# A fused transformer block on one core: second token blocks four pieces later, first halves' tiles ahead, and engines that may hold longer for urgent work

## The chip, the core and the metric

One core of a Trainium2 chip. The metric is the device time of one execution in microseconds (us), as the median of several. Six things work side by side on the core: TensorE (PE, with its weight loads as PEld), VectorE (DVE), ScalarE (ACT), GpSimd (POOL), SyncE (SP) and the DMA queues.

## The reference, cut to what matters

```python
x = A_x                                             # [1, 2048, 1024] bf16
h = x + linear_attention(layernorm(x), A_wqkv, A_wo)   # 32 heads, phi(t) = (t > 0 ? t + 1 : exp(t)) + 1e-6
g, u = layernorm(h) @ W_gate, layernorm(h) @ W_up      # F = 3584
h2 = h + (g * (g > 0) * u) @ W_down
```

## The kernel before

The big products are done in quads: seven products of half-size blocks in place of eight, from sums of blocks (the "left sums" of activations, sums of weights, sums of results). TensorE has 4163 matmuls; DVE and ACT move results out of PSUM, the memory that TensorE writes ("evict" them), make the sums and the norms; POOL scales and shifts normalised tiles; the SP queue transposes them by DMA. Tokens come in tiles of 128. `s` is the block of tokens, `i` the half, `tt` the tile in it. Tiles T0 to T7 belong to the first blocks, T8 to T15 to the second.

The program first records every instruction as a node, then a list scheduler lays them out ahead of time with estimated durations (`hold`), and they are issued in that order. Each engine then runs its own list strictly in order. `late` is the latest start that does no harm.

```python
# Plan.schedule(): the next engine to be free, and its most urgent ready instruction i
now = [i for i in a if nodes[i].ready <= s]
i = min(now, key=lambda i: (nodes[i].nom if e == "tensor" else nodes[i].late, i))
v = nodes[i]
if e != "tensor":
    soon = [j for j in a if s < nodes[j].ready < s + 0.5 * v.hold and nodes[j].late < v.late - 1500.0]
    if soon:                       # hold the engine for something more urgent
        i = min(soon, key=lambda j: (nodes[j].late, j))
        v = nodes[i]
        s = v.ready
v.start = s
clock[e] = s + v.hold
# ... (ends, DMA and successors: cut)

tiles = [Tile_(s, i, tt) for s in range(NS) for tt in range(SW // P) for i in range(2)]
# ... (steps() and the first blocks: cut)
t8, t9 = tiles[NTS:NTS + 2]
tick.units.extend([t8.nd01, None, t9.nd01, None, t8.nd2, t9.nd2] + steps(NTS, 2 * NTS, 2, 0, False)[4:])

def finish(self, on_dve=False):    # of a tile of the first norm
    self.rstd_()
    (nc.vector if on_dve else nc.gpsimd).tensor_scalar(out=xn, in0=self.x, scalar1=self.negm[:], scalar2=self.rstd[:],
                            op0=ALU.add, op1=ALU.mult)
    nc.sync.dma_start_transpose(out=XI[self.i][:, :, self.r:self.r + P], in_=xn)
```

`tick.units` is the list of pieces of attention work (`nd01`, `nd2`, `wo`) that are woven between the matmuls of the quads; a `None` is an empty turn.

## Time and profile before

| | before |
|---|---|
| median of 3 runs | 727.81 us (727.63 to 728.01) |
| the execution that was profiled | 726.09 us, span 724.3 us |
| PE busy | 714.4 us, 99% of the span |
| PE idle in its main group | 6.5 us |
| DVE, ACT, POOL busy | 563.9, 277.3, 77.8 us |

PE is nearly always busy, so the whole question is the handful of places where it isn't. The prediction below shows those lines; in a line of PE's timeline, the number in the brackets is how long PE stood idle before the stretch and the name after the arrow is what released it. The execution that was profiled took 1.7 us less than the median.

### The profile page before, as it was taken

The page shows a single profiled execution, that of the slowest core. Times are in us where ns is not written, and L with a number is a line of the kernel's source. Part 1 is how long each engine was busy: PE and PEld are TensorE (multiplying, and loading weights), DVE is VectorE, ACT ScalarE, POOL GpSimd, SP SyncE. Part 2 cuts the span into 40 slices and gives each one's busy share as a digit, 9 for nine tenths or more (in the row PEclk, how much of TensorE's full clock was granted, in tenths as well). Part 3 has the DMA queues.
Part 4 walks back from the last instruction along what each step waited for, and adds up shares of the span by engine and source line. Part 5 has one row for each costly group of instructions (what it writes and reads, how often), then busy time and mean ns, then how long its engine had stood idle before and what let it go on. Part 6 is the DMA issues. An engine that isn't in the chain of part 4 may idle for free.

```text
span 724.3 us, 11221 instructions
## 1 busy us (share of the span) xinstructions
PE 714.4 (99%) x4163; PEld 396.7 (55%) x4163; DVE 563.9 (78%) x954; ACT 277.3 (38%) x540; POOL 77.8 (11%) x88
## 2 busy tenths in 40 slices
PE   8999999999999999999999999999999999999998
PEld 4444545444444444444444444444444688888887
DVE  7897745887796885666767968769758879899996
ACT  5877555666554443333333333333333220001100
POOL 1342000002202110000000000000000004001452
PEclk9999999999999999999999999999999999999999
DMA  9556406069766630446145575685681878777974
GB/s 300 165 117 110 138 0 212 23 109 216 160 156 151 140 73 6 129 136 186 60 139 188 165 244 157 202 253 186 198 262 51 276 265 209 216 265 238 242 80 60
DMA packets 156503, 117.40 MB, mean 162 GB/s; under 512 B 54944, under 2 KB 140192, under 8 KB 156320
## 3 DMA queue, kind: packets, MB, share of 16 engines
q1 hardware_dynamic: 148832, 113.01, 53.9%
q0 software_dynamic: 7616, 3.67, 4.8%
q8 instruction: 32, 0.52, 0.3%
q14 instruction: 23, 0.19, 0.1%
HBM read 70.52 MB, written 34.08 MB: 144 GB/s over the span
## 4 chain that ended last, share of the span: by engine, by line
PE 85%; DVE 2%; DMA 2%; ACT 1%; issue 0%; POOL 0%; ACTq 0%
PE psum L122 85%; DVE mem L122 2%; DMA mem<-mem 2%; ACT mem L122 1%; POOL mem L122 0%; ACT tiny L122 0%; DVE tiny L122 0%; ACTq L122 0%
## 5 line engine op out<-in xcount | busy, mean ns | idle before, releaser
L122 PE MATMUL psum<-mem 128*128 128x512 f16 (+4 forms) x4147 | 713.3, 334 | 6.5 <-ACT mem L122 2.7
L122 PEld LDWEIGHTS <-mem 128*128 128x128 f16 (+1 forms) x4163 | 396.7, 98 | 323.8 <-issue 8.0
L122 DVE TENSOR_TENSOR mem<-psum,mem 128x512 f32<-128x512 f32 (+2 forms) x240 | 187.4, 794 | 99.3 <-ACT mem L122 65.1
L122 DVE TENSOR_TENSOR mem<-mem 128x512 f16<-128x512 bf16 (+8 forms) x400 | 241.6, 643 | 14.9 <-DMA mem<-mem 9.6
L122 ACT COPY mem<-psum 128x512 f32<-128x512 f32 (+2 forms) x124 | 92.7, 749 | 209.4 <-PE psum L122 197.9
L122 ACT COPY psum<-psum 128x512 f32<-128x512 f32 (+1 forms) x68 | 49.1, 722 | 160.3 <-PE psum L122 147.6
L122 POOL DMA_DIRECT2D out_dram<-mem x28 | 34.1, 1299 | 413.8 <-DVE mem L122 413.7
L122 ACT ACTIVATE mem<-psum 128x512 bf16<-128x512 f32 x90 | 53.6, 598 | 18.5 <-PE psum L122 18.0
L122 DVE SCALAR_TENSOR_TENSOR mem<-mem 128x512 bf16<-128x512 bf16 (+1 forms) x71 | 57.7, 813 | 1.3
L122 POOL TENSOR_SCALAR mem<-mem,tiny 128x1024 bf16<-128x1024 bf16 x28 | 37.5, 1338 | 196.9 <-ACT tiny L122 176.8
L122 DVE SCALAR_TENSOR_TENSOR mem<-psum,mem 128x512 bf16<-128x512 f32 x66 | 45.4, 688 | 11.9 <-PE psum L122 7.9
L122 ACT ACTIVATE mem<-mem,tiny 128x1024 bf16<-128x1024 bf16 x24 | 27.4, 1143 | 11.0 <-DVE tiny L122 5.8
L122 DVE TENSOR_SCALAR mem<-mem 128x512 bf16<-128x512 bf16 (+1 forms) x49 | 16.3, 332 | 17.6 <-ACT mem L122 17.4
L122 DVE TENSOR_TENSOR mem<-psum,tiny 128x384 bf16<-128x384 f32 (+1 forms) x48 | 22.9, 508 | 5.3 <-ACT tiny L122 3.9
L122 ACT ACTIVATE mem<-mem 128x1024 bf16<-128x1024 f32 (+1 forms) x23 | 24.3, 1056 | 6.5 <-DVE mem L122 6.4
L122 ACT ACTIVATE tiny<-tiny 128x1 f32<-128x1 f32 (+2 forms) x112 | 22.8, 206 | 7.5 <-DVE tiny L122 4.7
L122 ACT ACTIVATE tiny<-psum 128x12 f32<-128x12 f32 (+1 forms) x48 | 8.1, 169 | 13.9 <-PE psum L122 13.4
L122 DVE BATCH_NORM_STATS2 tiny<-mem 128x6 f32<-128x512 bf16 x16 | 10.2, 682 | 2.5 <-DMA mem<-in_A_x_dram 2.5
L122 ACT CAST mem<-psum 128x512 bf16<-128x512 f32 x18 | 10.4, 582 | 4.2 <-PE psum L122 3.7
L122 POOL TENSOR_SCALAR tiny<-tiny 128x1 f32<-128x1 f32 x14 | 4.7, 337 | 25.2 <-ACT mem L122 13.3
L122 ACT ACTIVATION_READ_ACCUMULATOR mem<-mem,tiny 128x1 f32 x24 | 4.5, 188 | 0.0
L122 DVE TENSOR_SCALAR tiny<-tiny 128x1 f32<-128x1 f32 x16 | 3.4, 210 | 0.3
(18 smaller groups left out, 14.4 us busy)
## 6 DMA issues: line engine op xcount, KB each, us to landing
l_dram<-mem SPq DMA_DIRECT2D x98, 128.0 KB, 2.2
mem<-l_dram SPq DMA_DIRECT2D x12, 896.0 KB, 6.4
mem<-in_A_x_dram SPq DMA_DIRECT2D x32, 256.0 KB, 3.0
mem<-in_B_W_up_dram SPq DMA_DIRECT2D x14, 512.0 KB, 5.3
mem<-in_B_W_gate_dram SPq DMA_DIRECT2D x14, 512.0 KB, 4.3
mem<-in_B_W_down_dram SPq DMA_DIRECT2D x28, 256.0 KB, 3.4
r_dram<-mem SPq DMA_DIRECT2D x56, 128.0 KB, 1.8
mem<-r_dram SPq DMA_DIRECT2D x8, 896.0 KB, 5.0
```

What stands on the lines that cost most here:

```text
L122: call = lambda: getattr(getattr(self.nc, eng), op)(*args, **k)
```

## The change

The intent: PE's waits are to go. Three edits, all to the order of work and none to the work. (1) Before 215 us of planned time an engine other than TensorE may be held, that is kept idle, for up to 1.2 times the length of the instruction it would start, not 0.5, where something more urgent is nearly ready. (2) The tiles of the first blocks go half by half. (3) The attention pieces of the second blocks start four turns later.

```diff
+    SHORT = 215000.0
...
-                soon = [j for j in a if s < nodes[j].ready < s + 0.5 * v.hold and nodes[j].late < v.late - 1500.0]
+                wait = (1.2 if s < self.SHORT else 0.5) * v.hold
+                soon = [j for j in a if s < nodes[j].ready < s + wait and nodes[j].late < v.late - 1500.0]
...
-    tiles = [Tile_(s, i, tt) for s in range(NS) for tt in range(SW // P) for i in range(2)]
+    tiles = [Tile_(0, i, tt) for i in range(2) for tt in range(SW // P)]
+    tiles += [Tile_(1, i, tt) for tt in range(SW // P) for i in range(2)]
...
-    tick.units.extend([t8.nd01, None, t9.nd01, None, t8.nd2, t9.nd2] + steps(NTS, 2 * NTS, 2, 0, False)[4:])
+    tick.units.extend([None] * 4 + [t8.nd01, None, t9.nd01, None, t8.nd2, t9.nd2] + steps(NTS, 2 * NTS, 2, 0, False)[4:])
```

## The prediction

> **What bounds the kernel now.** I read the page first, then the timeline of PE, then the busy time by stretch, then the short timelines of ACT and DVE around each gap of PE. The page:
>
> ```profile
> PE 714.4 (99%) x4163; PEld 396.7 (55%) x4163; DVE 563.9 (78%) x954; ACT 277.3 (38%) x540; POOL 77.8 (11%) x88
> ...
> L122 PE MATMUL psum<-mem 128*128 128x512 f16 (+4 forms) x4147 | 713.3, 334 | 6.5 <-ACT mem L122 2.7
> ```
>
> PE is busy 99% of a span of 724.3 us, and the chain that ended last is 85% PE. But "busy" with modelled ends may hide slack, so I check the pace: from 285 to 570 us the stretch view counts 1322 matmuls of 512 columns in 285.0 us, 215.6 ns each. Start to start, the trace has 215 or 216 ns for 512 columns, 109 for 256, 57 to 62 for 132. Taking each form's median as its pace, the 4163 matmuls need 709.9 us; first to last start they took 719.4. So only some 9.6 us of PE time are lost at all, 2.9 of them in the first 10 us. The timeline of PE (start, length, and in brackets idle before and its releaser) shows where:
>
> ```profile
> 28.76 25.68 PE L122 MATMUL psum<-mem 128*128 128x512 bf16 x140 [0.54 <-DVE mem L122]
> 55.01 94.85 PE L122 MATMUL psum<-mem 128*128 128x512 f16 x518 [0.57 <-ACT mem L122]
> 150.64 40.70 PE L122 MATMUL psum<-mem 128*128 128x512 bf16 x219 [0.78 <-DMA mem<-mem]
> 192.79 9.26 PE L122 MATMUL psum<-mem 128*128 128x512 bf16 x48 [1.46 <-ACT mem L122]
> 202.61 97.68 PE L122 MATMUL psum<-mem 128*128 128x132 bf16 x489 [0.56 <-DVE mem L122]
> ```
>
> Start to start the same five cost 0.70, 0.73, 0.94, 1.62 and 0.72 us (a matmul's modelled tail covers some 0.16 of each). Smaller hitches add 0.9 between 40 and 77 us, 0.3 at 127, 0.4 at 146 and 0.6 between 205 and 208. After 208.5 us PE runs at its pace to the end: nothing later can be gained, only lost. The stretches say what is full beside PE:
>
> ```profile
> 140.00:152.00 12.00, 11.16 (x67) 5.53 (x66) 11.76 (x24) 7.56 (x25) 0.00 (x0) 1.00 0.24 45
> 152.00:188.00 36.00, 36.00 (x199) 17.67 (x198) 26.23 (x67) 20.55 (x67) 8.87 (x7) 1.00 0.89 185
> 188.00:210.00 22.00, 19.82 (x108) 9.34 (x106) 20.55 (x41) 16.08 (x41) 1.19 (x1) 1.00 0.67 167
> 210.00:285.00 75.00, 75.00 (x378) 35.24 (x377) 58.03 (x117) 31.48 (x89) 9.81 (x8) 1.00 0.45 98
> ```
>
> The columns after the length are PE, PEld, DVE, ACT, POOL. Where PE loses time DVE is at 98% and 93%; between them it has 27% to spare. The short timelines tell the worst gap:
>
> ```profile
> 187.93 0.42 DVE L122 TENSOR_TENSOR mem<-mem 128x512 f16<-128x512 bf16 x1 [2.76 <-DMA mem<-mem]
> ...
> 189.60 1.06 ACT L122 ACTIVATE mem<-mem 128x1024 bf16<-128x1024 f32 x1 [1.15 <-DVE mem L122]
> 190.56 1.14 ACT L122 ACTIVATE mem<-mem,tiny 128x1024 bf16<-128x1024 bf16 x1
> ...
> 192.17 0.57 ACT L122 COPY mem<-psum 128x512 f32<-128x512 f32 x1
> ```
>
> DVE stood 2.76 us before a left-sum instruction whose transpose had not landed, with a PSUM eviction ready behind it; then ACT did a 1.06 us exponential and a 1.14 us square while the copy PE wanted (its products were done at 190.4) waited until 192.17.
>
> **What the Trainium skill says.** "TensorE: Matmul & The Clock Gate", section "Wait — 56ns, not 53.3ns?": N/2.4 GHz plus about 2.5 ns start to start when warm, 215.7 ns at 512 columns, 426.7 when cold. The trace agrees: 215 to 216, and about 427 for the first eight, so PE's pace can't be improved by this change. "Perfetto Trace Analysis", section "Identifying the Most-Contended Engine": PE busy time is a poor measure of how near PE is to its limit; hence the count by pace. Same page, section "Sequencer Loop": an instruction waits for its semaphores before it executes; the trace shows the consequence in the 2.76 us above, an engine waiting for one instruction with ready work behind it. "DMA: Bandwidth & Descriptors", section "Latency and other measured facts", gives about 2 us as the fixed cost of a DMA, growing with load; here transposes took 3.1 us (the one PE waits for at 150.64) and 5.0 us (182.95 to 187.9, with the DMA busy).
>
> **The change, part by part.** No matmul, eviction or transfer is added: the built programs have the same 4163 matmuls and 663 DVE rows in other orders. It all happens in the scheduler that orders instructions ahead of time. I compared the built orders and set the order of before against the trace by counting.
>
> (1) Before the scheduler's own 215 us, a non-PE engine may now hold up to 1.2 times an instruction's length, not 0.5, when something more urgent is about to be ready. At 28.76 PE waits for an add from PSUM (0.69 us at 28.02) behind two statistics instructions (1.28 us) that nobody needs soon; the new order has the add first. Gain: the whole 0.70. At 55.01 PE waits for an ACT copy (54.39) behind two tiny instructions which waited for DVE; the new order has the copy ahead of them. Gain 0.73. The hitches of 40 to 77 us: same kinds, some go and some new ones come; I take 0.2. At 192.79 the new order is copy, square, two tiny, exponential, copy for PE, with the 1.06 us exponential behind it. Chain from the durations: the square of the last first-half tile can start after the copy ending 188.45; 1.14 + 0.19, two tiny 0.44, the exponential from PSUM 0.58, the copy 0.57: about 191.4 to 191.5 with overheads. PE wants it at 191.1. So the gap goes from 1.62 to about 0.4: gain 1.2.
>
> (2) First halves' tiles ahead. The left sums of the first blocks need both halves, so they move back behind the last eviction (in the new DVE order both evictions of the last tile precede them). The 2.76 us stand is avoided: the last tile is evicted about 1.3 us sooner, so its normalised tile is transposed sooner (before: issue at 194.91; by the ACT chain above, 190.3 for the tiny, 1.2 on POOL, so some 191.6: 3 us sooner). But seven of eight left sums of that group (0.42 or 0.69 us each) now bunch between 188 and 200.
>
> (3) Four pieces further. The first attention group of the second blocks comes some 28 matmuls later (6 us), and the rest of it follows after the gate quad's first products. This takes three normalising evictions (0.55 us each) out of DVE's full stretch and spreads the load. In exchange the product that needs the full left sums, before at 203.65 just 0.3 us after they were ready at 203.34, now comes near 199. Adding DVE's new order from 187 by the durations above (four sums of 0.69, one phi of 0.29 + 0.69, adds 0.69, joins 0.42 + 1.22, sums 0.42), these sums end at about 199.5 to 200, so I expect 0.3 to 0.7 of wait there, and 0.2 to 0.4 at two of the next attention pieces, whose three PSUM banks DVE must free. Against 1.3 us lost from 201 to 208 before, I take a gain of 0.3.
>
> (4) At 150.64 PE waits for the transpose of the first attention output, issued at 147.48, when DVE had evicted it at 147.45. In the new order a 0.28 us clamp and a 0.68 us sum no longer stand ahead of that eviction; but the PE work in between is the same. Gain 0.4 of 0.94.
>
> Sum: 0.70 + 0.73 + 0.2 + 1.2 + 0.3 + 0.4 = 3.5 us. Off the path: the end of the second blocks' tiles slides by 16 matmuls (3.5 us) against the gate work; their sums were done at 272.8 and first used at 282.4, so about 6 us of slack stay: cost 0. I give 0.5 back for new hitches where DVE is over 90% and nothing was measured. Net 3.0: 727.8 to **724.8 us**.
>
> **Rivals.** (a) DVE becomes the bound from 188 to 210: 93% busy, now with bunched sums; a wait of 1 to 2 us for left sums takes the place of the 1.46. For it: a slack of 0.3 us before and a product that moves 4 us earlier. Against it: 2.76 us of stand freed on the same engine. Time 726 to 727. (b) A hold is idle time by choice, planned with estimated durations; where the urgent instruction comes late, DVE or ACT stands still with work at hand, in stretches where they are 80% busy. For it: nearly all orders before 77 us change. Against it: PE's statistics for these tiles have several us of slack (the last one's transpose, 69.49, feeds sums used near 100). Time 727 to 729. (c) All waits of the stretch go, 6.5 us in all: 721.5. Against it: POOL, transposes and the DVE load don't change. (d) The gained time is hidden anyway: excluded, since PE runs at pace after 208.5 and no other engine holds the end.
>
> **Range and chances.** Floor 721.5 by (c), ceiling about 729 by (b). The 2% line is 14.6 us away: the whole loss from 10 us on is 6.7, so faster by over 2% is impossible by this count, and slower by over 2% would take a stall larger than any here. 8 in 10: 722.8 to 727.4.
>
> **What would show it.** In the changed profile: PE idle in its group falls from 6.5 to about 3.5; no gap at 28 or 54; one of 0.2 to 0.5 near 191; a short one near 199 to 202 released by DVE; DVE's 2.76 us stand at 185 gone; PE still without gaps after 215. It would be wrong if a new PE gap over 1 us shows near 199 (rival a), if small gaps multiply before 80 (rival b), or if PE loses its pace between 215 and 285.

## The result, and the profile after

| | before | after |
|---|---|---|
| median | 727.81 us (5 runs, 727.06 to 728.07) | 726.78 us (5 runs, 726.60 to 727.46) |
| ratio of the fast runs | | 0.9991, 95% interval 0.9977 to 1.0004: the same within 2% |
| profiled execution, span | 724.3 us | 724.8 us |

A ratio is the mean time of one kernel's fast runs over that of the other's in the same rounds, so it isn't quite the ratio of the medians. By the ratio the change took 0.7 us off, by the medians 1.0, and the interval does not even exclude nothing; 3.0 were predicted. The two lines of the page of the changed kernel that answer to those shown of before:

```profile
PE 711.6 (98%) x4112; PEld 397.0 (55%) x4163; DVE 565.5 (78%) x954; ACT 276.9 (38%) x540; POOL 81.5 (11%) x88
...
L123 PE MATMUL psum<-mem 128*128 128x512 bf16 (+4 forms) x4096 | 710.7, 334 | 9.8 <-ACT mem L123 2.6
```

Read the counts first. There are 4163 weight loads but 4112 matmuls: 51 matmul records are missing from this trace, and each leaves a hole that looks like an idle PE. So the 9.8 us are not comparable with the 6.5 before. What can be compared are single waits, in PE's timeline of the changed kernel:

```profile
30.29 25.34 PE L123 MATMUL psum<-mem 128*128 128x512 bf16 x137 [1.40 <-DVE mem L123]
57.55 94.02 PE L123 MATMUL psum<-mem 128*128 128x512 f16 x509 [1.92 <-ACT mem L123]
152.16 19.52 PE L123 MATMUL psum<-mem 128*128 128x512 bf16 x110 [0.59 <-DMA mem<-mem]
172.03 4.95 PE L123 MATMUL psum<-mem 128*128 128x512 bf16 x27 [0.34 <-DVE mem L123]
177.32 30.66 PE L123 MATMUL psum<-mem 128*128 128x512 bf16 x149 [0.34 <-DVE mem L123]
208.20 91.99 PE L123 MATMUL psum<-mem 128*128 128x512 f16 x453 [0.23 <-ACT psum L123]
```

The stretch view (after the length: PE, PEld, DVE, ACT, POOL):

```profile
152.00:188.00 36.00, 34.89 (x187) 17.02 (x192) 28.61 (x69) 20.30 (x67) 7.49 (x7) 1.00 0.83 180
188.00:210.00 22.00, 21.62 (x109) 10.21 (x110) 20.15 (x39) 14.76 (x33) 2.14 (x2) 1.00 0.69 172
```

From 188 to 210 us PE is busy for 21.62 us, where it was 19.82, with DVE at 20.15 for 20.55. The late wait of 1.46 us at 192.79 is gone, and 202.61's 0.56 has become 0.23. Two new ones of 0.34 stand at 172 and 177. But the two early waits, which were to vanish, are 1.40 and 1.92 us, where before's profile had 0.54 and 0.57. Where do they come from? Three lines of DVE's timeline of the changed kernel:

```profile
20.42 3.49 DVE L123 TENSOR_TENSOR mem<-mem 128x512 f16<-128x512 bf16 x5 [1.91 <-DMA mem<-mem]
...
24.77 4.66 DVE L123 TENSOR_TENSOR mem<-mem 128x2048 f16<-128x2048 bf16 x4
...
29.56 0.68 DVE L123 TENSOR_TENSOR mem<-psum,mem 128x512 f32<-128x512 f32 x1
```

DVE was held 1.91 us for left sums whose transpose had not landed. The sums of weights that it might have done in that time come after (1.22 us each, but for the last, which took 2.06 us beside a normalisation on POOL), and the add that PE waits for, at 29.56, is behind them; in the first profile of before it came at 28.02. ACT and POOL of the changed kernel before the second wait:

```profile
54.97 1.15 ACT L123 ACTIVATE mem<-mem,tiny 128x1024 bf16<-128x1024 bf16 x1 [1.94 <-POOL tiny L123]
56.92 0.58 ACT L123 COPY mem<-psum 128x512 f32<-128x512 f32 x1
...
50.38 4.38 POOL L123 TENSOR_SCALAR mem<-mem,tiny 128x1024 bf16<-128x1024 bf16 x2
54.73 0.21 POOL L123 TENSOR_SCALAR tiny<-tiny 128x1 f32<-128x1 f32 x1
```

PE wants the copy at 56.92. ACT's list has a square before it, the square needs a 128x1 negation on POOL (54.73), and POOL reaches that only after two normalisations that took 4.38 us together. A single such normalisation can take 1.19 us, so these two lost 2 us somewhere. The experiments say where.

**A measure for all runs.** To compare the runs I took, from each trace, the start-to-start time of PE's matmuls beyond their pace (216 ns at 512 columns, 109 at 256, 60 at 132), summed over gaps of more than 60 ns, from the first matmul behind the second group of transposes at about 10.5 us. A gap within 7 ns of 212 ns over the pace is taken for a missing record and left out. I call it the loss, and split it at 120 and 180 us into early, middle and late. The rule also drops real waits of about 0.2 us: in the first profile of before, which misses no record, it drops two, at 76.56 and 146.04 us, and in the first of after one at 194.91. A wait of 0.20 near 146 us is counted in e14 and e18 alone, so differences of 0.2 between two figures of the table say nothing.

### The profile page after: what moved, and what is told of

Same layout as the page of the kernel before. It is cut to its first block, busy times and chain, and to the rows that moved or that the text cites. A ratio compares the mean times of both kernels' runs of the same rounds, so it can differ in the third digit from the quotient of the medians.

```text
span 724.8 us, 11177 instructions
## 1 busy us (share of the span) xinstructions
PE 711.6 (98%) x4112; PEld 397.0 (55%) x4163; DVE 565.5 (78%) x954; ACT 276.9 (38%) x540; POOL 81.5 (11%) x88
## 4 chain that ended last, share of the span: by engine, by line
PE 87%; ACT 2%; DVE 2%; issue 1%; DMA 0%; POOL 0%; ACTq 0%; DVEq 0%
PE psum L123 87%; DVE mem L123 1%; ACT mem L123 1%; DMA mem<-mem 0%; ACT tiny L123 0%; ACT psum L123 0%; DVE tiny L123 0%; POOL tiny L123 0%; ACTq L123 0%; DVEq L123 0%
## 5 line engine op out<-in xcount | busy, mean ns | idle before, releaser
L123 PE MATMUL psum<-mem 128*128 128x512 bf16 (+4 forms) x4096 | 710.7, 334 | 9.8 <-ACT mem L123 2.6
L123 POOL TENSOR_SCALAR mem<-mem,tiny 128x1024 bf16<-128x1024 bf16 x28 | 40.8, 1457 | 181.7 <-ACT tiny L123 172.2
L123 DVE TENSOR_SCALAR mem<-mem,tiny 128x1024 bf16<-128x1024 bf16 x4 | 2.2, 546 | 2.4 <-ACT tiny L123 1.8
```

What stands on the lines that cost most here:

```text
L123: call = lambda: getattr(getattr(self.nc, eng), op)(*args, **k)
```

## The experiments

There were eighteen runs, and all their results were correct. The kernels of one call share the runs of before; its medians were 727.61 and 727.65 (e1 to e8), 727.57 (e9 to e12, the same chip), 727.29 (e13 to e16, a second chip) and 727.23 us (e17, e18, a third). Between calls, ratios are to be compared and not medians. All in one table first; the single experiments follow. "Norms on DVE" means that the twelve normalisations of the first norm that POOL ran are on DVE; a hitch is a small wait of PE, of under 0.7 us.

| run | edit | median us (runs) | ratio to before | loss early / middle / late, us | sum |
|---|---|---|---|---|---|
| before, first profile | | 727.81 | | 2.25 / 1.42 / 3.03 | 6.71 |
| e5 | before, again | 727.92 (1) | | 3.50 / 1.43 / 2.91 | 7.84 |
| after, first profile | whole change | 726.78 (5) | 0.9991 | 3.79 / 2.22 / 0.69 | 6.70 |
| e9 | whole change, again | 727.04 (5) | 0.9994 | 3.77 / 2.21 / 0.96 | 6.94 |
| e1 | hold alone | 728.05 (5) | 1.0006 | 3.74 / 2.20 / 2.10 | 8.05 |
| e2 | order and move, no hold | 727.07 (5) | 0.9993 | 3.04 / 1.44 / 2.12 | 6.60 |
| e3 | order, move, hold from 80 us | 726.54 (5) | 0.9985 | 3.60 / 2.20 / 0.86 | 6.66 |
| e4 | order, move, hold to 80 us | 727.34 (5) | 0.9995 | 3.77 / 1.42 / 2.12 | 7.32 |
| e6 | order alone | 726.27 (4) | 0.9982 | 3.14 / 1.46 / 1.68 | 6.28 |
| e16 | order alone, again | 725.47 (5) | 0.9979 | 2.54 / 1.44 / 1.68 | 5.65 |
| e7 | move alone | 727.43 (6) | 0.9999 | 3.29 / 1.42 / 2.93 | 7.64 |
| e8 | hold from 80 us alone | 727.36 (5) | 0.9999 | 3.01 / 2.23 / 2.10 | 7.34 |
| e10 | order, hold from 80 us | 727.72 (5) | 1.0004 | 3.17 / 2.21 / 2.09 | 7.46 |
| e11 | order, one norm on DVE | 726.70 (5) | 0.9991 | 3.29 / 1.44 / 1.68 | 6.40 |
| e12 | order, norms on DVE | 725.71 (5) | 0.9977 | 2.17 / 1.63 / 1.69 | 5.49 |
| e13 | whole change, norms on DVE | 724.97 (5) | 0.9967 | 2.13 / 2.09 / 0.85 | 5.08 |
| e14 | order, move, hold from 180 us | 725.42 (5) | 0.9972 | 3.19 / 1.63 / 0.86 | 5.68 |
| e15 | e14, norms on DVE | 724.62 (5) | 0.9964 | 2.28 / 1.56 / 0.86 | 4.69 |
| e17 | e15, hold to 80 us too | 723.97 (5) | 0.9959 | 2.11 / 1.29 / 0.86 | 4.26 |
| e18 | before, norms on DVE | 726.78 (5) | 0.9995 | 2.35 / 2.08 / 3.17 | 7.59 |

The loss is read from one profiled execution, so it has that execution's luck in it; the medians have less. The 95% interval of a ratio is about 0.0013 to each side, 0.9 us, so single differences of some tenths rest on the losses and not on the times. The start, before 10.5 us, varies from run to run and is in the medians and not in the loss.

### e1 to e4: which part is worth what

Theory: the longer hold gains late and loses early. e1 undoes the order and the move and keeps the hold; e2 undoes the hold; e3 and e4 keep the order and the move, and the hold only late or only early.

```diff
# e1: the old list of tiles, and without [None] * 4
# e2
+                wait = 0.5 * v.hold
# e3
+                wait = (1.2 if 80000.0 < s < self.SHORT else 0.5) * v.hold
# e4
+                wait = (1.2 if s < 80000.0 else 0.5) * v.hold
```

> The longer hold alone, tile order and the four pieces undone. Theory (the hold costs early: the two early PE gaps grow from 0.70 and 0.73 us to 1.6 and 2.1 us start to start): both large early gaps, about 1.5 and 2 us, are in this profile too, and the time is 1 to 2.5 us above before, 728.5 to 730. Rival (tile order or late pieces push the early work): early gaps as before, 0.7 each, and a time at or below before.

> The changed kernel with the short hold (0.5) everywhere; tile order and four pieces kept. Theory: early gaps back to 0.5 to 0.6 idle at 28 and 55 us, as before; what remains of the gain at 188 to 210 us tells what the reordering alone is worth, I expect 1 to 2.5 us less than before there and a time of 725.3 to 726.8. Rival (reordering needs the hold): gaps at 190 and 202 us come back and the time is that of before, 727.8.

> The longer hold only from 80 us of the scheduler's clock on; tile order and four pieces kept. The built PE order is that of the changed kernel, the early orders are those of before. Theory: early gaps 0.5 to 0.6 idle, late ones as in the changed kernel (0.2 to 0.6 each), time 2.2 us below the changed kernel, 724.3 to 725. Rival (the early loss is not the hold's doing): within 0.5 us of the changed kernel, 726.8.

> The longer hold only up to 80 us of the scheduler's clock. Theory: gaps of 1.4 and 1.9 idle at 30 and 57 us, and the late stretch as without the hold: 2.2 us above the kernel with no longer hold anywhere. Rival: within 0.5 us of it.

Measured: 728.05, 727.07, 726.54 and 727.34 us, beside 727.61 for before. The sign is that of the theory: by the medians the early hold costs 0.27 us (e4 less e2) and the late one gains 0.53 (e3 less e2), both within the noise. Its size isn't, and no time lies in its theory's range: e3 and e4 are where their rivals had them, within 0.5 us of the changed kernel and of e2. e1 does show the two large early waits (loss 3.74). Comparing the first two profiles, the early part of the changed kernel had lost 1.5 us more than that of before (3.79 less 2.25). And e2 and e3, which have no early hold, show 3.04 and 3.60 us of early loss, not 2.25. So either the first profile of before was no typical one, or something else is wrong. The hold alone (e1) gains nothing at all, which the prediction had given 2.8 of its 3.5 us.

### e5: the profile of before once more

> The kernel before, profiled once more. Theory (the first profile of it was an unusually quick execution): that execution took 726.09 us where the median is 727.6, so a second profile, of an execution near 727.5, shows an idle time before the stretch near 55 us of about 1.4 us in place of 0.57, or a wait for a weight load near 10 us of 0.3 to 0.9 us that the first profile had not, together 1 us or more. Rival (the early waits are a property of the order and of nothing else): the same two idle times as in the first profile, 0.54 near 28 us and 0.57 near 55 us to within 0.15 us, and no wait near 10 us; then what the comparison of the two first profiles says of the early hold, some 2 us lost, has to be explained against the timed runs in another way.

The theory held. PE's timeline of before, second profile (an execution of 727.92 us):

```profile
29.65 25.68 PE L122 MATMUL psum<-mem 128*128 128x512 bf16 x137 [0.50 <-DVE mem L122]
56.78 21.50 PE L122 MATMUL psum<-mem 128*128 128x512 f16 x118 [1.45 <-ACT mem L122]
...
194.63 9.26 PE L122 MATMUL psum<-mem 128*128 128x512 bf16 x48 [1.33 <-ACT mem L122]
```

The same program, the same lists, and the wait at 55 to 57 us is 1.45 us, not 0.57. Two lines of each trace tell why. First profile of before, DVE then POOL:

```profile
52.16 0.42 DVE L122 TENSOR_TENSOR mem<-mem 128x512 f16<-128x512 bf16 x1
...
51.99 1.48 POOL L122 TENSOR_SCALAR mem<-mem,tiny 128x1024 bf16<-128x1024 bf16 x1 [2.55 <-issue]
```

Second profile of before, the same two instructions:

```profile
53.05 1.29 DVE L122 TENSOR_TENSOR mem<-mem 128x512 f16<-128x512 bf16 x1
...
52.88 1.19 POOL L122 TENSOR_SCALAR mem<-mem,tiny 128x1024 bf16<-128x1024 bf16 x1 [2.54 <-issue]
```

A left sum on DVE (two inputs in SBUF) and a normalisation on POOL (reads SBUF) meet, and one of them waits for the other: either POOL takes 1.48 us in place of 1.19, or DVE takes 1.29 in place of 0.42. The 0.87 us that DVE then loses go straight through its list into the statistics, the ACT instructions behind them and the copy that PE waits for (0.57 + 0.87 = 1.44; measured 1.45). The Trainium skill has this: "SBUF — State Buffer", section "Who interferes with whom", says that a DVE instruction with two SBUF inputs contends with a GpSimd instruction that reads SBUF, that the port pair they share is an exclusive lock, and that issue order decides which of the two is blocked. The trace agrees that one blocks the other and doesn't share. It doesn't show who was first: POOL's recorded start is 0.17 us ahead of DVE's in both profiles.

In the ten profiled executions of programs whose lists have this meeting the left sum took 0.42 us in two (before's first, e16) and 1.29 or 1.30 in eight (e2, e3, e5, e6, e7, e8, e10, e14). Two programs show both outcomes: before, and the order alone (e6, e16). The prediction was read off one of the two.

### e6, e7, e8: each part alone

```diff
# e6: the new list of tiles only     # e7: [None] * 4 only     # e8: only
+                wait = (1.2 if 80000.0 < s < self.SHORT else 0.5) * v.hold
```

> The new order of the tiles alone; hold 0.5 everywhere, the units of the second blocks not moved. The order and the move together took 0.54 us off (727.61 to 727.07). Theory 1 (the order does it, since it moves the copy that the 1.46 us wait at 192.79 stood for): 727.0 to 727.2, and the wait near 193 of over 1 us is gone. Theory 2 (the four pieces do it): 727.5 to 727.7, and the wait near 193 of over 1 us is still there.

> The move by four pieces alone; hold 0.5 everywhere, the old order of the tiles. Theory 1 (the order does it): 727.5 to 727.7 with the wait near 193 of over 1 us still there. Theory 2 (the four pieces do it): 727.0 to 727.2 with that wait gone. If both of the two kernels are near 727.3, each gives half; if neither leaves 727.6, it takes both at once.

> The longer hold from 80 to 215 us alone, on the kernel before. Where the order and the move were in, the late hold took 0.53 us off. Theory 1 (the parts add): 727.61 - 0.53 = 727.1, and the wait near 193 falls from 1.46 us to about 0.2 as in the kernel with the hold alone everywhere. Theory 2 (the late hold needs the new order): 727.5 or more, since what leaves 193 returns near 204 and 213 (0.56 and 0.38 us in the kernel with the hold alone).

Order alone: 726.27 us, a larger gain than the 727.0 to 727.2 expected of it, and by the medians better than all three parts together (ratios 0.9982 and 0.9991, whose intervals overlap). Move alone: 727.43, next to nothing. Late hold alone: 727.36, also next to nothing; its theory of a sum of parts (727.1) was wrong. PE's timeline of the order alone:

```profile
56.43 94.63 PE L123 MATMUL psum<-mem 128*128 128x512 f16 x509 [1.45 <-ACT mem L123]
151.81 49.93 PE L123 MATMUL psum<-mem 128*128 128x512 bf16 x262 [0.75 <-DMA mem<-mem]
202.30 98.06 PE L123 MATMUL psum<-mem 128*128 128x132 bf16 x480 [0.56 <-DVE mem L123]
```

The wait near 193 is gone without any longer hold: late loss 1.68 for 2.91. ACT's timeline of the order alone shows the cause:

```profile
188.38 1.15 ACT L123 ACTIVATE mem<-mem,tiny 128x1024 bf16<-128x1024 bf16 x1 [2.29 <-DVE tiny L123]
...
191.77 0.57 ACT L123 COPY mem<-psum 128x512 f32<-128x512 f32 x1
```

The last square ahead of that copy is at 188.38, where before's first profile had it at 190.56. DVE no longer stands 2.76 us for a transpose ahead of the eviction that this square needs; between 183 and 188 us it stands 0.97 at most, and for PE. So ACT is through with the square before the copy is due. The copy is at 191.77 and PE loses 0.10 us there.

The hold from 80 us takes 0.8 from the late loss (2.91 to 2.10 in e8) and adds 0.8 to the middle (1.43 to 2.23). Those are the two waits at 172 and 177. DVE's timeline of the changed kernel before the second of them:

```profile
175.17 0.42 DVE L123 TENSOR_TENSOR mem<-psum,tiny 128x256 bf16<-128x256 f32 x1 [0.45 <-ACT tiny L123]
175.51 1.15 DVE L123 TENSOR_TENSOR mem<-mem 128x1024 f16<-128x1024 bf16 x1
176.58 0.68 DVE L123 SCALAR_TENSOR_TENSOR mem<-psum,mem 128x512 bf16<-128x512 f32 x1
```

DVE stands 0.45 us, does the piece it stood for, then a left sum of 1.15 us, and only then the eviction at 176.58 whose bank PE waits for: PE goes on at 177.32. In e14, without the hold there, the same eviction runs at 175.08, with no such sum between.

### e9 to e12: the changed kernel again, the order with the late hold, and the norms on DVE

e10 is e6 with the hold of e3. e11 and e12 move normalisations from POOL to DVE on top of e6, one of them (tile 13) or all twelve of the first norm that POOL had; the 16 of the second norm stay on POOL. (I wrote 14 in the expectation; the other two of the 14 are on DVE in every version. And "of the first blocks" is wrong there and below: they are of the first norm, of all 16 tiles of tokens. Tile 13 is the fourteenth of these 16.)

```diff
# e11: (13,)     # e12: range(16)
-            (nc.vector if on_dve else nc.gpsimd).tensor_scalar(
+            (nc.vector if on_dve or self.t in (13,) else nc.gpsimd).tensor_scalar(
```

> The changed kernel once more, beside the others on one chip. From start-to-start losses the profiles of before (the second one) and of after differ by 7.84 - 6.70 = 1.1 us. Theory (the order of the tiles alone gives the gain, the hold and the move give some of it back): the order alone stays ahead of it by 0.4 us, so 726.7 here where the order alone has 726.3. Rival (the 726.27 of the order alone was chance, four runs): the changed kernel is at 726.3 or less in these rounds.

> The new order of the tiles and the longer hold from 80 to 215 us, without the move by four pieces. Theory 1 (the late hold trades one wait for another: 0.18 us less near 150, two new ones of 0.5 near 171 and 176): 726.3 to 726.8, no better than the order alone. Theory 2 (the late hold also takes away the 0.72 and 0.27 us waits near 201 and 205): 725.3 to 725.9.

> The new order of the tiles, and one instruction moved: the normalisation of tile 13 (1024 wide) runs on VectorE for an estimated 0.37 us, and no longer on GpSimd, where it ran from 52.5 to 53.7 us while VectorE's last left sum took 1.29 us in place of 0.42. Theory (the two engines shut each other out there, and the wait of 1.61 us near 54.6 is what VectorE's lost 0.87 us and the copy queued behind it make): that left sum takes 0.42 us, the wait near 54.6 falls from 1.61 to 0.7 to 1.1 us, the time to 725.4 to 725.9. Rival (the left sum is slow for another reason, or the wait is bounded elsewhere): the wait stays at 1.5 us or more and the time at 726.2 or more.

> The new order of the tiles, and all 14 normalisations of the first blocks that GpSimd ran are on VectorE, an estimated 14 x 0.37 = 5.2 us more for it, while GpSimd keeps only 128x1 scalings. Theory (GpSimd's wide reads are what makes the early waits long): no left sum before 80 us takes over 0.5 us, the waits near 28 and 55 fall under 0.7 us each, the time is 725.0 to 725.7. Rival (VectorE, 48 of 60 us busy there, has no 5 us to spare): new waits for VectorE between 30 and 80 us, and 726.5 us or more.

e9: 727.04, and the same early waits as in the first profile (1.56 and 2.08 start to start). The order alone stays ahead by the medians. e10: 727.72. Neither theory: the late hold on the order alone doesn't only gain nothing, it costs 1.2 us of loss (0.75 in the middle, 0.41 late). It pays only with the move: with order and move, it takes the late loss from 2.12 to 0.86 (e2, e3). So the parts don't add; the move alone does nothing, on top of the order it costs 0.44 us late (1.68 to 2.12), and it pays with the hold.

e11 checks the meeting of DVE and POOL at 52 us by taking POOL's part away. DVE's timeline of e11:

```profile
53.39 0.42 DVE L123 TENSOR_TENSOR mem<-mem 128x512 f16<-128x512 bf16 x1
...
54.33 0.53 DVE L123 TENSOR_SCALAR mem<-mem,tiny 128x1024 bf16<-128x1024 bf16 x1
```

The left sum takes 0.42 us, as expected of the theory, and the wait falls from 1.61 to 1.19 us start to start. I had expected 0.7 to 1.1: the normalisation took 0.53 us on DVE, not the 0.37 I had estimated, and it lies on the same path (1.61 - 0.87 + 0.53 = 1.27). The time, 726.70, is a miss: a hitch of 0.44 at 65.8 us is new, the one at 71 grew from 0.22 to 0.68 and one of 0.25 went, which is 0.65 us more in all and took the gain back.

e12 moves all twelve: 725.71 us, the wait at 55 is 0.79 (under 0.7 expected) and the early loss 2.17, for 3.14 in e6. The rival, that DVE has no 6.5 us to spare (12 x 0.54), is refuted, though a wait of 0.60 near 82 and a longer one for the transpose near 150 (1.45, was 0.91) give 1.1 us back. All groups of DVE, then of POOL, in e12:

```profile
L123 DVE TENSOR_SCALAR mem<-mem,tiny 128x1024 bf16<-128x1024 bf16 x16 | 8.5, 543 | 4.8 <-ACT tiny L123 3.7 <-issue 1.0
...
L123 POOL TENSOR_SCALAR mem<-mem,tiny 128x1024 bf16<-128x1024 bf16 x16 | 19.4, 1210 | 174.9 <-ACT tiny L123 171.0 <-DVE mem L123 3.9
```

The same instruction costs 543 ns on DVE and 1210 on POOL. The Trainium skill, "GPSIMD Engine Reference", section "4.1 Engine selection", has elementwise work on a tile on VectorE, with one-input work on GpSimd "roughly line-rate". The measured factor is 2.2. The row doesn't say which rate it means.

### e13 to e16: does the early hold lose by itself, and where does the late one gain?

e13 is the whole change with e12's norms. e14 is the whole change with the hold only from 180 us, e15 the same with e12's norms. e16 repeats e6.

```diff
# e14, e15
+                wait = (1.2 if 180000.0 < s < self.SHORT else 0.5) * v.hold
```

> The whole change, with the first blocks' normalisations on VectorE in place of GpSimd. Theory (the early waits of the changed kernel, 1.56 us near 28.5 and 2.08 near 55, are made longer by the two engines shutting each other out; the longer hold itself is then worth something): both fall under 0.8 us and the time is 725.0 to 725.7. Rival (the early hold loses time whoever normalises): at least one of the two stays over 1.3 us, the time is 726.0 or more, and the order alone with VectorE's normalisations (725.71) stays the better.

> Order of the tiles, move by four pieces, and the longer hold only from 180 to 215 us. Theory (of the late hold only the part after 180 us gains; before it, it makes two waits of 0.51 us near 171 and 176 for 0.2 us less near 150): those two are gone, the waits near 205 and 214 (0.78 and 0.63 us without any hold) fall to the 0.39 us near 208 that the changed kernel has, sum of losses 5.2 to 5.8 us, time 725.6 to 726.2. Rival (what is held after 180 us needs the orders that the hold makes before): waits over 1.2 us in all after 200, time 726.5 or more.

> The same as the one before it with the normalisations on VectorE. Theory (parts add: the normalisations took 0.8 us off the losses, 6.28 to 5.49): 724.7 to 725.4, the fastest so far. Rival (they share a limit): 725.6 or more, no better than the order alone with VectorE's normalisations.

> The order of the tiles alone, once more, five runs. Theory (it alone gives the gain): 726.0 to 726.6, ratio near 0.998. Rival (its 726.27, from four runs, was chance): 727.0 or more, no better than the whole change in its 10 runs (726.8 to 727.0).

e13: 724.97 us. Two lines of PE's timeline, and the line of DVE's where DVE is held:

```profile
30.00 26.30 PE L123 MATMUL psum<-mem 128*128 128x512 bf16 x141 [1.04 <-DVE mem L123]
56.99 92.96 PE L123 MATMUL psum<-mem 128*128 128x512 bf16 x505 [0.69 <-DVE mem L123]
...
20.53 3.49 DVE L123 TENSOR_TENSOR mem<-mem 128x512 f16<-128x512 bf16 x5 [2.23 <-DMA mem<-mem]
```

The early loss of the whole change falls from 3.79 to 2.13, and it is now no more than without an early hold (2.17 in e12, 2.28 in e15; one profile each). So the early hold has a net cost only together with POOL's normalisations. Neither of its two waits fell under the 0.8 us expected: the one from 28.6 on is still 1.20 us start to start (1.56 before), since DVE is still held there, 2.23 us, for the same transpose; the one from 55.9 on is 0.85, for 2.08. The edit takes away two things at once, the meetings of the two engines and POOL's queue ahead of the negation that ACT needs; no run tells them apart. In return the hitches between 40 and 85 us go: 0.08 us, for 0.82 without the hold in e12.

e14: 725.42 us. The waits at 172 and 177 are gone, the one at 206 stays at 0.39, and the late loss is 0.86, as in e3. So the hold gains after 180 us and needs no hold before it (that it needs the move, e10 suggests, with the hold from 80 us). e15: 724.62, by the ratios not clear of e14. e16: 725.47, under the 726.0 to 726.6 expected, and the gain of the order is confirmed: its two ratios, 0.9982 and 0.9979, have intervals below 1, and its profile happened on the other outcome of the meeting at 52 us (early loss 2.54 for 3.14 in e6).

### e17, e18: both ends, and the norms alone

```diff
# e17, on e15
+                wait = (1.2 if s < 80000.0 or 180000.0 < s < self.SHORT else 0.5) * v.hold
# e18: before, with e12's edit alone
```

> All normalisations on VectorE, order and move in, the longer hold up to 80 us and from 180 to 215 us, not between. Theory (the waits of 0.51 us near 170 and 175 come from the hold between 80 and 180 us, and with VectorE normalising the early hold costs nothing): those two are gone, the early waits are those of the kernel with the hold throughout and VectorE's normalisations (1.20 + 0.85), sum of losses 4.1 to 4.6 us, time 724.2 to 724.8. Rival (the early hold still costs, or what it moves returns later): the sum is 4.8 us or more and the time 724.9 or more, behind the kernel with the hold from 180 us only (724.62).

> The kernel before with nothing changed but the engine of the first blocks' normalisations, VectorE in place of GpSimd. Theory (what it gains has nothing to do with the change): its early waits are as with the new order, 0.5 to 0.9 us near 28 and 55, the wait near 193 of 1.5 us is still there, and the time falls by 0.6 to 1.2 us, to 726.1 to 726.8. Rival (it only repairs what the change made worse): less than 0.4 us, 727.0 or more.

e17: 723.97 us, ratio 0.9959 (0.9945 to 0.9972), the fastest, 3.3 us under before in the same rounds; its lead over e15 (0.9964) is within the noise of the times. Loss 4.26, as expected; the time is a little under the 724.2 expected. Its page and PE's timeline, with all 4163 records this time:

```profile
L123 PE MATMUL psum<-mem 128*128 128x512 bf16 (+4 forms) x4147 | 713.5, 335 | 4.9 <-DVE mem L123 1.7
```

```profile
30.03 26.25 PE L123 MATMUL psum<-mem 128*128 128x512 bf16 x144 [1.01 <-DVE mem L123]
56.98 93.29 PE L123 MATMUL psum<-mem 128*128 128x512 bf16 x514 [0.69 <-DVE mem L123]
151.22 54.54 PE L123 MATMUL psum<-mem 128*128 128x512 bf16 x292 [0.95 <-DMA mem<-mem]
205.99 94.36 PE L123 MATMUL psum<-mem 128*128 128x512 f16 x472 [0.23 <-ACT psum L123]
```

Four waits of over 0.3 us are left. e18: 726.78, between the theory (726.1 to 726.8 by 0.6 to 1.2 us) and its rival; the gain of 0.45 us in the same rounds is less than expected. The early loss does fall as in the other versions, 3.50 to 2.35, so the exclusion was there before the change as well. But the wait for the first attention output's transpose near 150 grows from 0.94 to 1.70, and that near 192 from 1.49 to 1.75. Why the transpose doesn't come earlier with PE was not tested.

## Why the prediction was wrong, point by point

The class (within 2%) and the range (722.8 to 727.4) held; the gain was 0.5 to 1.0 us (e9's medians and the first ones) where 3.0 were predicted. In losses, from the second profile of before to the first of after: 7.84 to 6.70, or 1.14.

- **The term that failed: step (1), the early gains of 0.70 + 0.73 + 0.2 = 1.63 us.** Measured early loss 3.50 before and 3.79 after, -0.29. "The gap at 28.76 gone" became a wait of 1.56, "the gap at 55.01 gone" one of 2.08. Only the hitches went, and by more than the 0.2: 1.23 us in e5, 0.14 after. By the times of e2 and e4 the cost of the early hold is within the noise; that it gains nothing is clear. The prediction took the order of a list for its timing: the add and the copy did move ahead of the instructions named, but the holds that moved them left DVE standing 1.91 us, and bunched POOL's normalisations against DVE's sums (the pair of 4.38 us is there in e1, e4 and e9, which have the early hold, and not in e2 and e3). e13 shows that without the second the early hold costs nothing on balance (2.13 us, for 2.17 without it). Rival (b) named the first half of this and gave it 727 to 729; its sign was small gaps that multiply before 80 us, where the two large ones grew.
- **The gap at 54 to 57 was also mis-sized before the change.** 0.57 us idle was the rarer outcome, of two of the ten profiles with this meeting; about 1.45 is what the other eight show. A gain of 0.73 could not have been the right size even had the wait gone.
- **Step (1), 1.2 us at 192.79: right in size, wrong in cause.** The wait went from 1.49 to 0.21 (at 194.91, one of those that the measure drops) and to 0.26 in e9, and DVE's stand of 2.76 at 185 is gone too. But the order alone does this (e6), by what step (2) says of it, an earlier eviction of the last tile. The hold alone also cures that wait, to 0.38 (e8), and pays for it at 172 and 177.
- **Steps (2) and (3), 0.3, with new waits of 0.3 to 0.7 near 199 to 202.** None is there. What is left near 201 to 208 is 0.39 us, for 1.31 before, a gain of 0.9. But order and move alone (e2) leave 1.59 us between 205 and 215, and the late hold on top of them 0.39 (e3): what the prediction gave to (2) and (3) here is the hold's, as what it gave to the hold at 192.79 is the order's.
- **Step (4), 0.4 at 150.64:** 0.94 to 0.75, so 0.2.
- **The 0.5 for new hitches where DVE is full:** 1.0 us, at 172 and 177, in a stretch that the prediction had not named.
- **The late half as a whole:** 1.2 + 0.3 + 0.4 - 0.5 = 1.4 predicted; middle and late measured 4.34 to 2.91, 1.43. The terms are off each way and the sum agrees, which is luck in part.
- **A sum in the text:** the floor of 721.5 us is 721.3 by its own figures (727.8 - 6.5); nothing rests on it.
- **What would show it:** "PE idle from 6.5 to 3.5" was a poor test: the figure was 9.8, but before's own second profile, with 51 records missing too, has 10.7. PE keeps its pace after 215 us but for one hitch of 0.20 at 270 (and one of 0.10 at 575 that before has too).

Left open: why POOL or DVE wins at 52 us in one execution and not in another; why a move that gains nothing alone is needed for the late hold to gain; and the wait at 150.

## What to carry to other kernels

Where a scheduler holds an engine for something nearly ready, judge the hold stretch by stretch on the chip: here, with the new order and the move in, the same rule gained 1.3 us of loss after 180 us, lost 0.8 between 80 and 180, and before 80 lost or did nothing depending on where a neighbour's work ran. Profile the kernel before more than once before its gaps are priced: one wait of 1.45 us read 0.57, and the profiled run's time, 1.7 us under the median, was a hint of it (against the second profile, half of the difference is a quicker start, 9.93 for 10.86 us). When two engines shut each other out, try the work on the one that does it faster, even if that one is the busier: here it took 0.9 to 1.7 us off the early loss in each of four pairs of profiles (e12, e13, e15, e18 against e6, after, e14, e5; against the two profiles with the other outcome at 52 us, e16 and before's first, 0.4 and nothing), but in the times it is clear of the noise only with the early hold in (e13, 0.9967, for 0.9991 and 0.9994).

## What the Trainium skill lacked or had wrong

- "SBUF — State Buffer", "Who interferes with whom": the rule holds (left sum 0.42 us alone, 1.29 behind POOL; normalisation 1.19 alone, 1.48 behind DVE). It lacks that the winner can change between executions of one program, as in before's two profiles and in those of the order alone, and that the recorded starts (POOL ahead by 0.17 us in both cases) don't tell which it was.
- "GPSIMD Engine Reference", "4.1 Engine selection": "roughly line-rate" for one-input work, which read alone would leave such work where it is. A 128x1024 bf16 tensor_scalar took 1210 ns on GpSimd and 543 on VectorE (means of 16 in e12).
- "Perfetto Trace Analysis", "Identifying the Most-Contended Engine": nothing there on missing records. With 51 of 4163 matmuls missing, PE's idle read 10.7 us in a profile of before where a full one read 6.5, though the losses of the two differ by 1.1 only; the weight loads, all 4163 present, give it away.
- No page that I read has a spread for the waits for a first weight load: 0 to 0.71 us in the profiles, just before the first matmul after the transposes, which began between 9.93 and 11.28 us. The rest of that spread has other parts, among them the 7 to 14 matmuls at the very start that took over 300 ns each where 216 is the pace.
